# The centring of tokens in tiles 2 and 3 moved one batch of scores later, and the GpSimd chain before it recorded with priority

## The chip, the cores and the metric

The kernel runs on one core of a Trainium2 chip. Its engines are TensorE (PE in the profile; PEld is its loading of weights), VectorE (DVE), ScalarE (ACT), GpSimd (POOL) and SyncE (SP), which issues nearly all DMAs. Each engine works through its own instructions in order, and semaphores tie the engines together. The metric is the device time of one execution in microseconds, the median over several runs.

## The reference

The input is 2048 tokens of width 512 in float32. Each token is normalised, and two branches read the result: attention with 32 heads of 16 over a sliding window of 256 tokens, and a gated feed-forward net of width 1792. They meet in a product, and the input is added.

```
x = A_x
xn = _layernorm(x, axis=-1)               # (x - mean) / sqrt(var + 1e-5)
s = _A_ref(xn, A_wqkv, A_wo)              # q, k, v; windowed softmax; @ wo
g = _silu(_B_ref(xn, B_w1, B_w3, B_w2))   # (silu(xn @ w1) * (xn @ w3)) @ w2
return x + s * g
```

The part that the change touches is the layer norm: mean, variance, the reciprocal root of the variance, and the subtraction and scaling (here "centring") of every token.

## The kernel before

**Tiles.** The tokens go in four tiles t = 0 to 3 of 512, each of four blocks b of 128 tokens. A large product runs as three products of f16 halves: XH and XL are the high and low part of the normalised tokens, turned so that the features lie on partitions. The work on attention is cut into 32 units (tile, group of 8 heads, half of the group). While unit n has its softmax and its values, unit n+2 has its row maxima; beside both, a list of pieces of the other products (projections of q and k, values, feed-forward, output) is spread between them.

**Batches.** `batches` makes five or four batches of scores for a unit. A batch records some score products with their maxima (`pass1`, L661 and L675: DVE adds the mask and takes the row maximum straight from PSUM) and some of `pass2` (L742, the mask added at L749 by DVE, the exponential at L752 by ACT, the values at L770). After each batch `spread` lets pieces of the other products follow, and `step` releases work that was put off by a count of steps (`later`).

**The layer norm of tiles 1 to 3** is made beside this, by `prepare(t)` and `prepare_beside`:

- `load(b)`: four DMAs of raw tokens (L433).
- `stats(b)`: DVE, mean and variance of a block (L437, L438) into `mv`.
- `rstd(0, 4)`: three small DVE instructions make a first guess `r0` (L442 to L447), and ten GpSimd instructions on 128x4 numbers refine it (L463 to L472). The last, L472, writes `rs`.
- `centre(b)`: DVE, one instruction of 128x512 for each block (L475), which reads `mv` and `rs`.
- `turn_beside(b, n, s)`: PE turns two quarters of a block into free columns of a score bank (L513), DVE makes XH and XL from it (L522, L523).

`prepare_beside` puts stats, rstd and centre into the list `behind`. Every batch with scores ahead takes one entry from it:

```
if behind and ahead:
    with tc.issue_after(lasts["maximum"].ins):
        behind.pop(0)()
```

So an entry stands behind the last row maximum of its batch. For tile 1 the entries are pairs of blocks; for tiles 2 and 3 they are four of stats, one of rstd, four of centre and one (`turns`) that lets the turning begin; that begins when a second call, from the list of pieces, has come as well.

**What sets the order.** PE's instructions stand as written. On the other engines the order follows the place where an instruction was recorded, unless it was recorded in `urgent()`, which is `tc.high_priority(offset=200)`: such an instruction stands as if it had been recorded earlier. What empties PSUM on DVE and ACT is recorded so: L614 (the low half of a projection, `rest` in `project`; ACT makes the high half at L610), L1281 (a sum of the down product into `ACC`), L1051 and L1056 (the two gates), L749, L675, L785. PSUM has two banks, called m, for all the large products; they take turns (`bank`), so the piece after next waits until DVE or ACT has emptied its bank.

**Other lines named later.** L1257 is PE's down product, L593 the projections of q and k, L563 values, L1032 gate and up. L339 and L841 on GpSimd are its larger instructions of 128x256: the product and the casts of the normalised attention output `on`, and halves of weights. L620 and L637 are DMAs of projections to and from DRAM, L705 DMAs of row maxima into `qa`, L358 the loading of wo.

## Time and profile before

| what | us |
|---|---|
| median of 3 runs | 818.14 (816.59 to 819.52) |
| the profiled execution, its own time | 817.82 |
| its span, first to last instruction | 816.0 |
| PE busy in the span | 795.2 (97%) |
| DVE busy | 633.9 (78%) |
| ACT busy | 392.4 (48%) |
| POOL busy | 364.0 (45%) |
| mean granted PE clock | 0.998 of full speed |

The profile is of one execution. Its page gives busy times and the chain of work that ended last; the view of waits gives for each line who ended its idle time; the timeline lists instructions in order of time, with the idle time before them in brackets; the view by windows gives for stretches of time the busy time of each engine, the granted clock and the share of the DMA engines in use. All times are counted from the start of the span. Line numbers are those of the kernel before; in the changed kernel the chain and the centring stand one line further down, and everything behind `prepare_beside` three.

### The profile page before, as it was taken

How to read it: one execution, taken by the hardware profiler on the slowest of the kernel's cores; microseconds unless marked ns; L12 is line 12 of the kernel's file. 1: busy time of each engine (PE TensorE's matmuls, PEld its weight loads, DVE VectorE, ACT ScalarE, POOL GpSimd, SP SyncE). 2: the span in 40 equal slices, each digit the busy share in tenths (PEclk: the TensorE clock that was granted, in tenths of full speed). 3: DMA queues.
4: the chain of work that ended last, by engine and by line, in shares of the span. 5: the costliest groups of instructions: out<-in, count | busy, mean ns of one | idle time of the engine just before them, and what ended most of it. 6: DMA issues, size and time to landing. Idle time of an engine off the chain costs nothing.

```text
span 816.0 us, 23868 instructions
## 1 busy us (share of the span) xinstructions
PE 795.2 (97%) x9176; PEld 404.2 (50%) x9176; DVE 633.9 (78%) x2037; ACT 392.4 (48%) x591; POOL 364.0 (45%) x648
## 2 busy tenths in 40 slices
PE   8999989998999999999999999999999999999998
PEld 4434444443444444444444544456544654466465
DVE  8788788885898777787988888786777887775437
ACT  6879586563527444444444344434444334344421
POOL 2234266232328636434445264630246377560670
PEclk9999999999999999999999999999999999999999
DMA  9967554735457384666755544646362545325321
GB/s 284 258 218 254 165 179 130 276 115 188 136 141 255 105 267 120 215 180 208 204 169 171 172 100 144 168 128 189 122 197 74 161 127 149 111 77 181 111 56 70
DMA packets 109794, 134.18 MB, mean 164 GB/s; under 512 B 18864, under 2 KB 64880, under 8 KB 109680
## 3 DMA queue, kind: packets, MB, share of 16 engines
q1 hardware_dynamic: 109392, 132.13, 53.9%
q8 instruction: 72, 1.18, 0.6%
q10 hardware_dynamic: 288, 0.52, 0.2%
q14 instruction: 42, 0.34, 0.1%
HBM read 91.23 MB, written 36.57 MB: 157 GB/s over the span
## 4 chain that ended last, share of the span: by engine, by line
PE 78%; DVE 10%; ACT 5%; DMA 3%; issue 3%; SPq 1%; POOL 1%; DVEq 0%; POOLq 0%; ACTq 0%
PE m L1032 29%; PE po L770 8%; PE m L1257 8%; PE m L1175 8%; PE m L593 7%; PE s L742 5%; PE m L1309 4%; PE m L563 4%; PE s L661 3%; DVE junk L675 2%; PE po L661 2%; DMA slot<-in_A_x_dram 1%; DMA dW<-slot 1%; DVE s L749 1%; ACT slot L342 1%
## 5 line engine op out<-in xcount | busy, mean ns | idle before, releaser
L1032 PE MATMUL m<-XH,slot 128*128 128x512 f16 x896 | 267.5, 380 | 1.8 <-DVE slot L614 1.2
L752 ACT ACTIVATE pt<-s,es 128x1024 f32<-128x1024 f32 x152 | 167.6, 1112 | 198.6 <-DVE s L749 183.1
L339 POOL TENSOR_TENSOR slot<-slot,slot 128x256 f16<-128x256 f32 (+1 forms) x170 | 112.9, 691 | 218.2 <-ACT slot L1065 79.2
L1032 PEld LDWEIGHTS <-slot 128*128 128x128 f16 x1344 | 124.8, 98 | 156.2 <-issue 12.7
L1032 PE MATMUL m<-XL,slot 128*128 128x512 f16 x448 | 169.9, 379 | 0.0
L749 DVE TENSOR_TENSOR s<-s,MK 128x256 f32<-128x256 f32 (+2 forms) x280 | 118.7, 434 | 52.7 <-PE s L742 48.5
L675 DVE CUSTOM_DVE_ANT_0 junk<-s,MW 128x320 bf16<-128x320 f32 x276 | 133.9, 485 | 18.0 <-PE s L661 10.3
L675 DVE CUSTOM_DVE_ANT_0 junk<-po,MW 128x320 bf16<-128x320 f32 x172 | 83.4, 485 | 4.3
L1257 PE MATMUL m<-slot,slot 128*128 128x512 f16 x336 | 80.0, 385 | 3.6 <-DVE slot L614 3.2
L770 PE MATMUL po<-pt,V 64*32 64x320 f32 (+4 forms) x2880 | 77.2, 342 | 0.8 <-DVE pp L304 0.8
L593 PE MATMUL m<-XH,slot 128*128 128x512 f16 x240 | 71.0, 380 | 1.5 <-DVE slot L1051 0.8
L1175 PE MATMUL m<-slot,slot 128*128 128x256 f16 x588 | 68.4, 273 | 0.0
L1090 POOL TENSOR_TENSOR slot<-slot,slot 128x256 f16<-128x256 f32 x98 | 64.6, 671 | 1.1
L1047 ACT ACTIVATE slot<-m,sgs 128x512 f32<-128x512 f32 x56 | 38.3, 683 | 54.4 <-PE m L1032 53.1
L770 PEld LDWEIGHTS po<-pt,V 64*32 64x32 f32 x2880 | 50.5, 106 | 22.9 <-PE s L513 0.9
L1175 PEld LDWEIGHTS <-slot 128*128 128x128 f16 x588 | 56.1, 98 | 11.5 <-issue 2.8
L1051 DVE SCALAR_TENSOR_TENSOR slot<-slot,m 128x512 f32<-128x512 f32 x56 | 38.4, 685 | 27.9 <-ACT slot L1047 27.8
L742 PE MATMUL s<-qa,KA 50*64 50x320 f16 (+3 forms) x1472 | 58.6, 260 | 0.3 <-DVE M L675 0.2
L593 PEld LDWEIGHTS <-slot 128*128 128x128 f16 x384 | 35.6, 98 | 44.7 <-issue 3.3
L742 PEld LDWEIGHTS <-KA 50*64 50x64 f16 x1472 | 30.3, 106 | 52.5 <-issue 31.1
L1257 PEld LDWEIGHTS <-slot 128*128 128x128 f16 x336 | 30.9, 98 | 42.7 <-issue 8.9
L661 PE MATMUL s<-KA,qa 48*64 48x320 f16 (+3 forms) x824 | 45.1, 295 | 3.7 <-ACT pt L752 2.9
(188 smaller groups left out, 1095.3 us busy)
## 6 DMA issues: line engine op xcount, KB each, us to landing
slot<-dW SPq DMA_DIRECT2D x98, 256.0 KB
slot<-in_B_w_dram SPq DMA_DIRECT2D x56, 256.0 KB
slot<-dFold SPq DMA_DIRECT2D x48, 256.0 KB
dW<-slot SPq DMA_DIRECT2D x42, 256.0 KB
slot<-in_A_x_dram SPq DMA_DIRECT2D x30, 256.0 KB
KA<-dK SPq DMA_DIRECT2D x24, 288.0 KB
qa<-dQ SPq DMA_DIRECT2D x32, 192.0 KB
slot<-dWQ SPq DMA_DIRECT2D x24, 256.0 KB
```

The lines of the kernel that those rows point to most:

```text
L339: op(out[:, c], a[:, c], b[:, c])
L593: nc.tensor.matmul(cell["pp"], w[:, (a * NC + c) * P:(a * NC + c + 1) * P], b[:, c, :], start=(c, i) == parts[0][0], stop=(c, i) == parts[ ...
L661: nc.tensor.matmul(s[c:c + w, r, :n], qa[rows, 2 * p + a, ii * P + c:ii * P + c + w], ka[rows, 2 * p + a, e - n:e], start=True, stop=True)
L675: lasts["maximum"] = nc.vector.tensor_tensor_reduce(out=junk[:, :n], in0=s[:, r, :n], in1=mask, scale=1.0, scalar=NEG, op0=ALU.add, op1=AL ...
L742: nc.tensor.matmul(s[64 * h:64 * h + 64, r, o:o + 64 * n], ka[rows, 2 * p + a, 64 * (m + 4):64 * (m + 5)], qa[rows, 2 * p + a, 64 * (m + k ...
L749: nc.vector.tensor_add(v, v, MK[:, kind, of:of + n, :].unsqueeze(1).to_broadcast([P, 2 * len(which), n, 64]))
L752: lasts["exp"] = nc.scalar.activation(pt, s, AF.Exp, scale=es)
L770: nc.tensor.matmul(cell["po"][32 * i:32 * i + 32, h, 64 * (m + k):64 * (m + k + n)], V[64 * h:64 * h + 64, (4 * t + m // 2) % VB, hd * VW: ...
L1032: nc.tensor.matmul(cell[k], w[:, (a * NC + c) * P:(a * NC + c + 1) * P], b[:, c, :], start=c == 0 and i == 0, stop=c == NC - 1 and i == 2)
L1090: nc.gpsimd.tensor_sub(lo, view, hi)
L1175: nc.tensor.matmul(cell["ps"][:, c], made[:, f:f + P], wj[:, g:g + 256], start=j == j0 and c == 0 and n == 0, stop=j == j1 - 1 and n == 2, ...
L1257: nc.tensor.matmul(ps, hh[:, a * TW + b * P:a * TW + (b + 1) * P], w[:, c * D:(c + 1) * D], start=f == f0 and i == 0, stop=f == f1 - 1 and ...
```

## The change

Two edits in the layer norm of tiles 1 to 3. The ten GpSimd instructions of `rstd` are recorded in `urgent()`. And for tiles 2 and 3 an empty entry stands in `behind` after rstd, so that each of the four centrings and `turns` are taken one batch later. No instruction is added, removed or resized.

```diff
             u = lnpool.tile([P, b1 - b0], F32, name="u")
-            pool.tensor_mul(sq, r0, r0)
-            pool.tensor_mul(sq, sq, ve)
...
-            pool.tensor_mul(rs[:, b0:b1], sq, r0)
+            with urgent():
+                pool.tensor_mul(sq, r0, r0)
+                pool.tensor_mul(sq, sq, ve)
...
+                pool.tensor_mul(rs[:, b0:b1], sq, r0)
...
         work.append(lambda: rstd(0, 4))
+        if t > 1:
+            work.append(lambda: None)
         work += [lambda bs=bs: [centre(b) for b in bs] for bs in pairs]
```

The order of the instructions of PE, ACT and SP is the same in both kernels. On DVE the four centrings of tile 2 and the four of tile 3 stand later, and everything they pass moves up by one; nothing else moves. On GpSimd only the chain of tile 2 changes its place among its neighbours.

The first centring of tile 2 on DVE, before; slot_2653 is block 0 of the tokens, m_3188 the bank of a projection, m_3248 one of the down product:

```order
L675 ISA junk,M<-po,M_106 128x256
L675 ISA M 128x1
L475 TENSOR_SCALAR slot_2653<-slot_2653,mv,rs 128x512
L614 SCALAR_TENSOR_TENSOR slot_3243<-m_3188,slot_3243 128x512
L1281 SCALAR_TENSOR_TENSOR slot_1458<-m_3248,dsc,slot_1458 128x512
L749 TENSOR_TENSOR s<-s,MK 128x4x64
```

The centring stands between a row maximum and two instructions that empty the banks m. At the same place on DVE in the changed kernel (L617 is L614 of before, L1284 is L1281, L752 is L749, L678 is L675):

```order
L678 ISA junk,M<-po,M_106 128x256
L678 ISA M 128x1
L617 SCALAR_TENSOR_TENSOR slot_3242<-m_3188,slot_3242 128x512
L1284 SCALAR_TENSOR_TENSOR slot_1458<-m_3247,dsc,slot_1458 128x512
L752 TENSOR_TENSOR s<-s,MK 128x4x64
```

The two follow the maximum directly. The centring stands one batch later, where that of block 1 stood before:

```order
L678 ISA junk,M<-po,MW 128x320
L678 ISA M 128x1
L476 TENSOR_SCALAR slot_2653<-slot_2653,mv,rs 128x512
L752 TENSOR_TENSOR s<-s,MK 128x4x64
L678 ISA junk,M<-s,MW 128x320
```

Blocks 1 and 2 likewise take the places of blocks 2 and 3. The last one, block 3 (slot_2659), stood here on DVE before, inside a few small instructions on a scale `al`:

```order
L675 ISA junk,M<-s,MW 128x320
L675 ISA M 128x1
L294 TENSOR_SCALAR al<-s 128x3
L475 TENSOR_SCALAR slot_2659<-slot_2659,mv,rs 128x512
L295 SCALAR_TENSOR_TENSOR al<-s,al 128x3
L785 COPY os<-po 128x512
```

and stands now thirteen rows further on, the one place that had no centring before:

```order
L752 TENSOR_TENSOR s<-s,MK 128x2x64
L678 ISA junk,M<-s,MW 128x320
L678 ISA M 128x1
L298 TENSOR_SCALAR al<-al 128x3
L476 TENSOR_SCALAR slot_2659<-slot_2659,mv,rs 128x512
L304 TENSOR_SCALAR pp_3394<-al 128x3
```

In tile 3 the four move in the same way: the first leaves its place, three take the place of the next, and the fourth comes to stand ahead of L687.

The chain of tile 2 on GpSimd before, from its fourth instruction on; `on` is a normalised attention output:

```order
L466 TENSOR_TENSOR sq<-sq,u 128x4
L339 TENSOR_TENSOR on<-on,rb 128x256 x2
L467 TENSOR_SCALAR sq<-sq 128x4
L841 CAST slot_3259<-on 128x256
L468 TENSOR_TENSOR r_3152<-r_3152,sq 128x4
L841 CAST slot_3259<-on 128x256
L469 TENSOR_TENSOR sq<-r_3152 128x4
L339 TENSOR_TENSOR slot_3259<-on,slot_3259 128x256
L470 TENSOR_TENSOR sq<-sq,ve 128x4
L339 TENSOR_TENSOR slot_3259<-on,slot_3259 128x256
L471 TENSOR_SCALAR sq<-sq 128x4
L472 TENSOR_TENSOR rs<-sq,r_3152 128x4
```

and in the changed kernel (the chain is L464 to L473, L844 is L841 of before):

```order
L339 TENSOR_TENSOR on<-on,rb 128x256
L468 TENSOR_SCALAR sq<-sq 128x4
L339 TENSOR_TENSOR on<-on,rb 128x256
L469 TENSOR_TENSOR r_3152<-r_3152,sq 128x4
L844 CAST slot_3258<-on 128x256
L470 TENSOR_TENSOR sq<-r_3152 128x4
L844 CAST slot_3258<-on 128x256
L471 TENSOR_TENSOR sq<-sq,ve 128x4
L339 TENSOR_TENSOR slot_3258<-on,slot_3258 128x256
L472 TENSOR_SCALAR sq<-sq 128x4
L339 TENSOR_TENSOR slot_3258<-on,slot_3258 128x256
L473 TENSOR_TENSOR rs<-sq,r_3152 128x4
```

Each large instruction has gone behind one instruction of the chain more, but all six still stand between the fourth instruction of the chain and its last, in both kernels. The chains of tiles 1 and 3 have kept their places.

More of the change, by code (lines that the diff above doesn't have):

```diff
@@ L462, in rstd @@
             u = lnpool.tile([P, b1 - b0], F32, name="u")
-            pool.tensor_mul(sq, r0, r0)
-            pool.tensor_mul(sq, sq, ve)
-            pool.tensor_scalar(u, sq, -10 / 3, None, op0=ALU.add)
-            pool.tensor_mul(sq, sq, u)
-            pool.tensor_scalar(sq, sq, 5.0, None, op0=ALU.add)
-            pool.tensor_mul(r0, r0, sq)
-            pool.tensor_mul(sq, r0, r0)
-            pool.tensor_mul(sq, sq, ve)
-            pool.tensor_scalar(sq, sq, -0.5 * (3 / 8)**3 * XS, 1.5 * (3 / 8) * XS, op0=ALU.mult, op1=ALU.add)
-            pool.tensor_mul(rs[:, b0:b1], sq, r0)
+            with urgent():
+                pool.tensor_mul(sq, r0, r0)
+                pool.tensor_mul(sq, sq, ve)
+                pool.tensor_scalar(u, sq, -10 / 3, None, op0=ALU.add)
+                pool.tensor_mul(sq, sq, u)
+                pool.tensor_scalar(sq, sq, 5.0, None, op0=ALU.add)
+                pool.tensor_mul(r0, r0, sq)
+                pool.tensor_mul(sq, r0, r0)
+                pool.tensor_mul(sq, sq, ve)
+                pool.tensor_scalar(sq, sq, -0.5 * (3 / 8)**3 * XS, 1.5 * (3 / 8) * XS, op0=ALU.mult, op1=ALU.add)
+                pool.tensor_mul(rs[:, b0:b1], sq, r0)
         def centre(b):
```

## The prediction

> **What bounds the kernel now.** The page first: TensorE (PE) is busy for nearly the whole span and fills most of the chain that ended last, so only what makes PE wait, or slows its clock, is worth anything.

> ```profile
> PE 795.2 (97%) x9176; PEld 404.2 (50%) x9176; DVE 633.9 (78%) x2037; ACT 392.4 (48%) x591; POOL 364.0 (45%) x648
> PE 78%; DVE 10%; ACT 5%; DMA 3%; issue 3%; SPq 1%; POOL 1%; DVEq 0%; POOLq 0%; ACTq 0%
> ```

> The view of waits says whom PE waits for (total, times, longest). I quote PE's two longest rows and the centring's own:

> ```profile
> PE m L1257 <- DVE slot L614: 3.2, 1, 3.2
> PE s L661 <- ACT pt L752: 2.9, 3, 1.6
> DVE slot L475 <- POOL rs L472: 3.8, 2, 3.4
> ```

> PE's longest single wait, 3.2 us, is for a projection's bank to be emptied by L614. And DVE has one wait of 3.4 us ahead of a centring. The timeline shows that the two are one event, in tile 2 (start, length, instruction, idle before):

> ```profile
> 184.60 0.20 POOL L463 TENSOR_TENSOR sq<-r 128x4 f32<-128x4 f32 x1 [8.11 <-DVE r L447]
> 185.80 1.42 POOL L339 TENSOR_TENSOR on<-on,rb 128x256 f32<-128x256 f32 x2
> 190.40 0.20 POOL L472 TENSOR_TENSOR rs<-sq,r 128x4 f32<-128x4 f32 x1
> 187.14 0.08 DVE L675 DVE_READ_ACCUMULATOR2_ANT M<- 128x1 f32 x1
> 190.63 0.55 DVE L475 TENSOR_SCALAR slot<-slot,mv,rs 128x512 f32<-128x512 f32 x1 [3.40 <-POOL rs L472]
> 191.09 0.68 DVE L614 SCALAR_TENSOR_TENSOR slot<-m,slot 128x512 f16<-128x512 f32 x1
> 187.09 0.59 ACT L610 ACTIVATE slot<-m 128x512 f16<-128x512 f32 x1
> 186.52 2.10 PE L1257 MATMUL m<-slot,slot 128*128 128x512 f16 x9
> 191.83 2.72 PE L1257 MATMUL m<-slot,slot 128*128 128x512 f16 x6 [3.20 <-DVE slot L614]
> ```

> GpSimd's chain ends at 190.60. DVE is free at 187.2 but has the centring next, waits for `rs`, and only then reaches L614, whose input from ACT was there at 187.68. PE has used up its other bank at 188.62 and stands until 191.83, when L614 has ended.

> The stall has a second price. Six of these products normally take 1.40 us, here 2.72; the rows below are from the chain of waits, the windows give busy times by engine, PE's granted clock and the DMA share:

> ```profile
> 85.48 1.40 PE m L1257 x6
> 191.83 2.72 PE m L1257 x6
> 194.55 0.57 PE s L742 x7
> 198.70 0.35 PE s L742 x8
> ```

> ```profile
> 191.20:191.80 0.60, 0.00 (x0) 0.00 (x0) 0.60 (x2) 0.00 (x0) 0.00 (x0) 0.80 0.04 10
> 191.80:194.50 2.70, 2.67 (x10) 0.74 (x9) 0.63 (x1) 0.00 (x0) 0.00 (x0) 0.50 0.67 232
> 195.20:196.00 0.80, 0.80 (x12) 0.36 (x5) 0.80 (x4) 0.00 (x0) 0.00 (x0) 1.00 0.95 351
> 54.00:57.00 3.00, 1.97 (x9) 0.68 (x7) 2.89 (x9) 2.90 (x7) 2.10 (x4) 1.00 0.73 249
> 55.64 0.59 PE L1032 MATMUL m<-XH,slot 128*128 128x512 f16 x2 [1.03 <-DVE slot L614]
> ```

> The granted clock falls to half only in the last part of the idle time (0.80 as a mean from 191.20 to 191.80) and is whole again from 195.20. A wait of 1.03 us at 55.64 left it at 1.00. [...]

> **The change part by part.**

> *Priority of the chain: nothing.* The ten small instructions keep all six large ones (on L339 and L841) ahead of the last, L472. I take `rs` to end at 190.60 as before; that GpSimd runs the six in a slightly other order moves the output of `on` by one small instruction, 0.2 us, and it is read only by the output product, units later. In tiles 1 and 3 the chain hasn't moved. So the first edit is worth 0.

> *First centring of tile 2, one batch later: the gain.* L614 no longer stands behind `rs`. It starts when ACT's half is there, 187.09 + 0.59 = 187.68. From the start of L614 to PE's start took 191.83 - 191.09 = 0.74, so the bank is free at 188.42. PE ends its nine products at 188.62 by the model. The wait of 3.20 is gone whole, with 0.2 us to spare; if the handover is worse than that by another 0.3, so much of the gain is lost. What then comes next on DVE, L1281, needs those nine products and stands at 188.6, as PE goes on.

> *The clock.* Without the idle time there is no half clock: 2.72 - 1.40 = 1.32 on the six products and 0.57 - 0.35 = 0.22 on L742 behind them, 1.54 together.

> *Where the centrings go.* The first now stands at the second one's old place, at 198.01:

> ```profile
> 198.01 0.54 DVE L475 TENSOR_SCALAR slot<-slot,mv,rs 128x512 f32<-128x512 f32 x1
> 201.67 0.54 DVE L475 TENSOR_SCALAR slot<-slot,mv,rs 128x512 f32<-128x512 f32 x1
> 209.12 0.63 DVE L298 TENSOR_SCALAR al<-al 128x3 int32<-128x3 int32 x1
> 216.80 0.69 DVE L614 SCALAR_TENSOR_TENSOR slot<-m,slot 128x512 f16<-128x512 f32 x1 [1.63 <-ACT slot L610]
> 203.50:215.00 11.50, 11.50 (x152) 5.73 (x145) 10.63 (x41) 6.33 (x10) 3.29 (x6) 1.00 0.32 86
> ```

> Shifted by the gain (3.20 + 1.54 = 4.74) that place is at 193.3, and `rs` was ready at 190.6: no wait, with 2.7 us to spare. Three of the four fill places that had a centring. The net addition is one centring behind L298, at 209.1 before the shift. It holds DVE 191.09 - 190.63 = 0.46 us, in a stretch where DVE is busy 10.63 of 11.50. Behind it are L1051 and L1056, which empty banks for PE; PE is busy 11.50 of 11.50 there, so it doesn't wait for either now, and at 216.80 DVE idles 1.63. Cost between 0 and 0.46; I take 0, since that idle time swallows it.

> *Tile 3.* Its chain isn't disturbed, and the centring doesn't wait:

> ```profile
> 409.09 0.20 POOL L472 TENSOR_TENSOR rs<-sq,r 128x4 f32<-128x4 f32 x1
> 410.69 0.54 DVE L475 TENSOR_SCALAR slot<-slot,mv,rs 128x512 f32<-128x512 f32 x1
> 428.03 0.30 DVE L687 TENSOR_SCALAR NM<-M 128x16 f16<-128x16 f32 x1
> 434.53 0.43 DVE L749 TENSOR_TENSOR s<-s,MK 128x256 f32<-128x256 f32 x1 [1.03 <-PE s L742]
> ```

> `rs` is there 1.4 us before the centring, so nothing is gained. The last centring now stands ahead of L687 and delays what follows by 0.46, until DVE's idle 1.03 at 434.5. Again 0 to 0.46, and I take 0.

> *The sum.* 817.82 (the profiled execution: span 816.0 and 1.82 around it) - 3.20 - 1.54 = 813.08. The median of the runs shown is 818.14, 0.32 above; with it **813.4**. From the bounds (0.3 of handover, twice 0.46) at worst 814.6 (813.4 + 0.3 + 0.92).

> **The rivals.**

> *A. Only the idle time is saved, about 814.9.* The half clock is seen in one execution, and there it set in just before the idle time was over; in other executions of before the same stall may have ended with the clock whole. The 1.54 was then not in the median, and what goes is 818.14 - 3.20 = 814.94. For: the three runs spread from 816.59 to 819.52, wider than 1.54. Against: the median is above the profiled execution, not 1.54 below. [...]

> *B. The wait moves to a transfer, about 817.8.* PE comes 4.7 us sooner to data that arrive at a fixed time. The issues just before the stall, and the share of the DMA engines after it:

> ```profile
> 186.41 2.77 SPq L705 DMA_DIRECT2D qa<-mt  x4
> 189.22 0.44 SPq L637 DMA_DIRECT2D qa<-dQ  x1
> 191.80 0.39 SPq L620 DMA_DIRECT2D dK<-slot  x1
> 194.24 1.99 SPq L358 DMA_DIRECT2D slot<-in_A_wo_dram  x4
> 198.60:203.50 4.90, 4.90 (x45) 2.18 (x44) 3.66 (x13) 3.10 (x5) 0.00 (x0) 1.00 0.83 297
> 206.97 0.34 PE s L742 x8
> ```

> The maxima and q for the next unit go out by 189.7, and PE reads them at 206.97, then at 202.2. If they came only at 207, nothing would be won. Against: they are ahead of the large block of transfers (L358 and what follows), with 12 us to go. That block itself is held up by L614 through L620 and moves ahead with PE. The same time would come out if the change didn't do what it says, that is if something else held L614 to 191.

> *C. Slower, about 824: the turning overtakes the centring.* PE's order hasn't moved, so each L513 (turning a block) stands where it stood, while the centrings come a batch later: from 198.01 to 201.67, 3.7 us. If the distance from a block's last instruction on DVE to its L513 were smaller than that, PE would stand about 3.7 us with the half clock's 1.54 behind it, 5.2 in each of two tiles: 818.14 - 4.74 + 10.4 = 823.8. It decides from the point where the distance is under one batch:

> ```profile
> 216.56 0.23 PE s L513 x16
> 441.39 0.42 DVE L522 CAST XH<-s 128x256 f16<-128x256 f32 x1
> ```

> Against it: the first L513 of tile 2 is at 216.56 and even the last centring stands at about 209.8 on the same scale; in tile 3 the first turned quarter is read at 441.39, the last centring stands at 428.

> **How the numbers follow.** Forecast 0.65, A 0.14, B 0.13, C 0.08 (with any other loss of more than the gain). A measurement of this kernel tells 0.3% from no change, about 2.5 us: faster is below 815.7. The forecast and most of A lie below: 0.76 faster. B and a badly measured rest of A give 0.16 for the same, C 0.08 for slower. The forecast's own range is 812.3 to 814.9. The range from 812.2 (the whole gain, and medians of three runs that spread by 2.9 us) to 816.4 takes in A and the upper ends of all costs, and leaves out C and most of B.

> **What would show it.** In the new profile: no wait of PE for the projection's L614 near 188, and no row of a centring's wait for `rs` over 1 us; granted clock 1.00 through 188 to 196, and a mean of 1.000 rather than 0.998; six products of L1257 in 1.40 there; the first centring near 193 without idle time ahead of it; L472 (then L473) still near 190.6; all later stages about 4.7 us sooner. I am wrong if PE stands elsewhere for over 1 us between 188 and 216, if it waits at an L513, or if the clock halves at another place.

## The result, and the profile after

| | us |
|---|---|
| before, median of 6 runs | 818.08 (816.59 to 819.52) |
| changed kernel, median of 6 runs | 813.25 (813.02 to 813.40) |
| ratio, with its 95% interval | 0.9938 (0.9928 to 0.9947) |
| the changed kernel's profiled execution, and its span | 813.03, 811.2 |

The change gained 4.83 us, and the runs agree far better than before. At the place of the old stall the timeline of the changed kernel reads as follows (start, length, instruction, idle before):

```profile
187.10 0.59 ACT L613 ACTIVATE slot<-m 128x512 f16<-128x512 f32 x1
187.73 0.69 DVE L617 SCALAR_TENSOR_TENSOR slot<-m,slot 128x512 f16<-128x512 f32 x1 [0.49 <-ACT slot L613]
188.68 0.75 DVE L1284 SCALAR_TENSOR_TENSOR slot<-m,dsc,slot 128x512 f32<-128x512 f32 x1 [0.26 <-PE m L1260]
186.53 3.40 PE L1260 MATMUL m<-slot,slot 128*128 128x512 f16 x15
190.40 0.20 POOL L473 TENSOR_TENSOR rs<-sq,r 128x4 f32<-128x4 f32 x1
193.17 0.54 DVE L476 TENSOR_SCALAR slot<-slot,mv,rs 128x512 f32<-128x512 f32 x1
204.83 0.53 DVE L476 TENSOR_SCALAR slot<-slot,mv,rs 128x512 f32<-128x512 f32 x1
```

L617, which empties the projection's bank, waits for ACT alone and starts at 187.73 instead of 191.09. PE runs its nine and the next six down products as one group of fifteen. GpSimd's chain ends as late as before, but the first centring comes only at 193.17 and doesn't wait. The granted clock (the number three from the right in the view by windows) stays whole:

```profile
189.00:190.00 1.00, 1.00 (x9) 0.34 (x11) 0.43 (x1) 0.00 (x0) 0.84 (x3) 1.00 0.02 4
191.00:192.00 1.00, 1.00 (x7) 0.41 (x6) 1.00 (x6) 0.59 (x1) 0.00 (x0) 1.00 1.02 336
193.00:194.00 1.00, 1.00 (x14) 0.38 (x15) 0.71 (x3) 0.09 (x1) 0.00 (x0) 1.00 0.98 219
```

In the view of waits the old first row of PE is gone, the second is now the first, and the longest wait of a centring is one of 0.4 us, in tile 1:

```profile
PE s L664 <- ACT pt L755: 2.9, 3, 1.6
DVE slot L476 <- POOL rs L473: 0.4, 1, 0.4
```

All of the gain is made at this one place: the nine products ahead of the stall start at 186.52 before and, in the group of fifteen, at 186.53 after. Near the end of the program, 24 products of the output projection, before and then after:

```profile
801.52 5.34 PE L1309 MATMUL m<-slot,slot 128*128 128x512 f16 x24
```

```profile
796.68 5.34 PE L1312 MATMUL m<-slot,slot 128*128 128x512 f16 x24
```

That is 4.84 us earlier; at the three products that follow the stall (195.29 before, 190.46 after) it was 4.83. Nothing was given back in the 600 us between.

### The profile page after: what moved, and what is told of

The parts are those of the page before. It is cut to its first block, busy times and chain, and to the rows that moved or that the text cites. A ratio compares the mean times of both kernels' runs of the same rounds, so it can differ in the third digit from the quotient of the medians.

```text
span 811.2 us, 23867 instructions
## 1 busy us (share of the span) xinstructions
PE 794.5 (98%) x9176; PEld 404.2 (50%) x9176; DVE 634.2 (78%) x2037; ACT 392.5 (48%) x591; POOL 364.0 (45%) x648
## 4 chain that ended last, share of the span: by engine, by line
PE 80%; DVE 9%; ACT 5%; issue 3%; DMA 2%; SPq 0%; DVEq 0%; POOL 0%; ACTq 0%
PE m L1035 30%; PE po L773 8%; PE m L1260 8%; PE m L1178 8%; PE m L596 7%; PE s L745 5%; PE m L1312 4%; PE m L566 4%; PE s L664 3%; DVE junk L678 2%; PE po L664 2%; ACT sqa L249 1%; ACT slot L342 1%; ACT pt L755 1%; DMA dW<-slot 1%
## 5 line engine op out<-in xcount | busy, mean ns | idle before, releaser
L755 ACT ACTIVATE pt<-s,es 128x1024 f32<-128x1024 f32 x152 | 167.7, 1113 | 192.8 <-DVE s L752 174.6
L339 POOL TENSOR_TENSOR slot<-slot,slot 128x256 f16<-128x256 f32 (+1 forms) x170 | 113.2, 694 | 212.2 <-ACT slot L1068 85.0
L752 DVE TENSOR_TENSOR s<-s,MK 128x256 f32<-128x256 f32 (+2 forms) x280 | 118.8, 435 | 50.7 <-PE s L745 46.4
L678 DVE CUSTOM_DVE_ANT_0 junk<-s,MW 128x320 bf16<-128x320 f32 x276 | 133.9, 485 | 18.0 <-PE s L664 10.3
L678 DVE CUSTOM_DVE_ANT_0 junk<-po,MW 128x320 bf16<-128x320 f32 x172 | 83.5, 485 | 4.3
```

Of the source, the lines that this page charges most:

```text
L339: op(out[:, c], a[:, c], b[:, c])
L678: lasts["maximum"] = nc.vector.tensor_tensor_reduce(out=junk[:, :n], in0=s[:, r, :n], in1=mask, scale=1.0, scalar=NEG, op0=ALU.add, op1=AL ...
L752: nc.vector.tensor_add(v, v, MK[:, kind, of:of + n, :].unsqueeze(1).to_broadcast([P, 2 * len(which), n, 64]))
L755: lasts["exp"] = nc.scalar.activation(pt, s, AF.Exp, scale=es)
```

## The experiments

The theories: (1) the wait of the first centring of tile 2, ahead of a bank's emptying in DVE's order, is the whole loss; (2) the priority brings part of the gain; (3) tile 3 brings part; and on the price of the stall, (1a) idle time costs itself and a half clock comes only behind a long one, against (1b) any such wait halves the clock.

**Each part of the change by itself.** The priority alone:

```diff
-            pool.tensor_mul(sq, r0, r0)
...
+            with urgent():
+                pool.tensor_mul(sq, r0, r0)
...
```

> The priority of the chain alone, centrings as before. Theory 1 (the first centring of tile 2 holds the bank's emptying back until rs is there): rs still ends near 190.4 us, PE waits about 3.2 us near 188 and the clock halves behind it; 818.1 us. Theory 2 (the priority brings part of the gain): between 813.3 and 817, with a shorter wait.

Measured: 818.05 us, ratio 1.0001 (0.9987 to 1.0015). `rs` ended at 190.72 and the stall was there:

```profile
190.52 0.20 POOL L473 TENSOR_TENSOR rs<-sq,r 128x4 f32<-128x4 f32 x1
191.96 1.94 PE L1258 MATMUL m<-slot,slot 128*128 128x512 f16 x6 [3.21 <-DVE slot L615]
```

The later centring alone:

```diff
         work.append(lambda: rstd(0, 4))
+        if t > 1:
+            work.append(lambda: None)
```

> The later centring alone, the chain without priority. Theory 1: all of the gain, 813.25 us, clock 1.000, no wait of PE near 188. Theory 2: some of the gain is missing, above 814 us.

Measured: 813.18 us, ratio 0.9941 (0.9922 to 0.9959). And in one tile each, `t == 2` and `t == 3` in place of `t > 1`:

> Later centring in tile 2 alone, no priority. Theory 1: 813.25 us. Theory 3 (tile 3's centrings bring a part as well): about 815 to 816 us. If tile 3's late centrings cost their 0.46 us, this is up to 0.46 faster than the change, 812.8.

> Later centring in tile 3 alone, no priority. Theory 1: as before, 818.1 us, with the same wait and half clock in tile 2. Theory 3: below 817 us.

Measured: tile 2 alone 813.15 us (0.9940, 0.9921 to 0.9959), tile 3 alone 818.29 us (1.0000, 0.9985 to 1.0015). Theories 2 and 3 fall: the priority alone leaves the wait and the time as they were, tile 3 brings nothing that these runs can tell, and the late centrings of tile 3 cost nothing that can be seen (813.18 with them, 813.15 without).

**Is it the lateness of rs, and not the centring's place?** Here the centring stays in front of the bank's emptying, and GpSimd's large instructions are moved from between the chain's steps to behind it:

```diff
-                later(3, multiply)
+                later(8 if (t, g) == (0, 1) else 3, multiply)
```

> Centrings where they were before, the chain without priority; instead the product of one attention output (its DMAs, the two large products, and so the casts and differences behind them) is put off by five steps, so that GpSimd has the chain of tile 2 without a large instruction in it. Theory 1 (the lateness of rs is the six large instructions): rs near 187.4 us instead of 190.6, PE waits 0.2 us or less, clock 1.000, 813.2 to 813.6 us, as fast as the change without moving a centring. Theory 4 (the position of the centring itself, its 0.46 us ahead of the bank's emptying, costs): about 813.7 us.

Measured: 813.30 us, ratio 0.9935 (0.9920 to 0.9949). The timeline of this kernel:

```profile
187.22 0.20 POOL L472 TENSOR_TENSOR rs<-sq,r 128x4 f32<-128x4 f32 x1
187.99 1.41 POOL L339 TENSOR_TENSOR on<-on,rb 128x256 f32<-128x256 f32 x2 [0.56 <-DMA qa<-mt]
187.46 0.55 DVE L475 TENSOR_SCALAR slot<-slot,mv,rs 128x512 f32<-128x512 f32 x1 [0.18 <-POOL rs L472]
186.57 3.54 PE L1257 MATMUL m<-slot,slot 128*128 128x512 f16 x15
```

The ten steps end 3.2 us sooner, and with them the stall ends, though no centring has moved. So the six large instructions inside the chain are what made `rs` late. This is the other cure, as fast as the change (their ranges, 813.09 to 813.49 and 813.02 to 813.40, overlap), and it is what the priority might be thought to do. Theory 4's 813.7 was missed: a centring in front of the bank's emptying costs nothing that can be told when it waits as little as here (0.18 us).

**The price of the stall.** Three kernels with the centrings as before and another length of chain. In the first, tile 2's second refinement is left out; the second adds one multiplication by 1 to that (its edit isn't shown); the third keeps the whole chain and adds six. The added lines of the first and the third:

```diff
+            if t == 2:
+                pool.tensor_scalar(rs[:, b0:b1], r0, (3 / 8) * XS, None, op0=ALU.mult)
+            else:
...
```

```diff
+            for _ in range(6 if t == 2 else 0):
+                pool.tensor_scalar(sq, sq, 1.0, None, op0=ALU.mult)
             pool.tensor_mul(rs[:, b0:b1], sq, r0)
```

> Centrings where they were before; in tile 2 the chain's second refinement is left out (four instructions become one scaling), so tile 2's normalisation is that of one step less. By the old rows rs ends near 188.64 instead of 190.60, PE's wait is about 1.3 us instead of 3.2. Theory 1a (idle time costs itself, a half clock comes only behind a long one): 813.25 + 1.3 = 814.5 us, clock 1.000, and runs that agree within 0.5 us. Theory 1b (any such wait brings the half clock, 1.5 us): 816.0 us.

> As the short chain, with one extra multiplication by 1 in it, which stands behind one more large instruction of GpSimd: rs near 189.4, PE's wait about 2.1 us. Theory 1a with a limit above 2.1: 815.3 us, clock 1.000, narrow spread. If the limit lies below 2.1: 816 to 818 us, with a spread of some us between runs, since the length of the half clock would depend on the moment.

> Centrings and chain as before, with six extra multiplications by 1 ahead of the chain's last instruction in tile 2: rs some 1.75 us later, PE's wait about 5.0 us. Idle time alone: 818.1 + 1.75 = 819.8 us if the clock's price stays what it was on average (1.6 us). If a longer wait makes the half clock surer or longer: up to 821.5 us. If the length of the half clock is a matter of the moment, the runs spread by 1 us or more, as before's do (816.59 to 819.52).

Their profiles give PE's wait, in this order:

```profile
190.73 1.46 PE L1260 MATMUL m<-slot,slot 128*128 128x512 f16 x6 [1.63 <-DVE slot L617]
```

```profile
191.25 2.28 PE L1262 MATMUL m<-slot,slot 128*128 128x512 f16 x6 [2.45 <-DVE slot L619]
```

```profile
193.45 2.72 PE L1259 MATMUL m<-slot,slot 128*128 128x512 f16 x6 [5.04 <-DVE slot L616]
```

The waits came out longer than I had worked out (1.63 for 1.3, 2.45 for 2.1). With the wait of 1.63 us the clock stayed whole at the stall and behind it:

```profile
188.00:192.00 4.00, 2.37 (x12) 0.87 (x9) 2.14 (x3) 0.16 (x1) 2.55 (x6) 1.00 0.25 83
192.00:196.00 4.00, 4.00 (x34) 1.73 (x33) 3.33 (x12) 1.12 (x1) 0.00 (x0) 1.00 0.95 309
```

Each execution also has its mean granted clock. A mean below 1.000 says that the clock was lower somewhere, not that it was at the stall: in this profiled execution (mean 0.999) the clock is 1.00 in every window of 20 us up to 800 us, and 0.92 only from 800 to 820, some 600 us behind the stall, and with tile 2 alone an execution of 813.06 us had a mean of 0.997. So the table gives the times beside the means; the row on before takes the 44 executions that ran beside the experiments:

| PE's wait in the profile | executions | times at a mean clock of 1.000 | times below that |
|---|---|---|---|
| none (the change, 6) | 6 | 813.03 to 813.30 | 813.02, 813.40 (0.999) |
| 1.63 | 6 | 814.99 | 815.07 to 815.50 (0.998, 0.999) |
| 2.45 | 12 | 7: 815.82 to 816.00 | 5: 816.13 to 819.40 |
| 3.20 (before) | 44 | 10: 816.34 to 817.21 | 34: 817.76 to 820.82 |
| 5.04 | 6 | none | 820.06 to 821.49 |

At 1.63 us the median is 815.12, 1.87 above the change: the idle time and little else, and theory 1b's 816.0 is missed by all six. At 2.45 the median is 815.94; seven executions kept the full clock, and four (817.36 to 819.40) stand at least 1.36 above them. The fifth, 816.13, lies so close to the seven that its half clock probably stood elsewhere; no profile shows it. At 3.20 time and mean go together: ten of 44 kept the full clock, and the 34 others begin 0.55 above the last of them. The median of the ten, 816.65, is 3.40 above the change, and that of the 34, 818.22, is 1.57 higher still. At 5.04 none kept it; the median, 820.58, is 0.8 above the 819.8 expected from the longer idle time alone. So 1a holds, but with no sharp limit: in these four kernels, the longer the wait, the surer the half clock (by the times, none of 6 executions, 4 or 5 of 12, 34 of 44, 6 of 6). Its middle price here, 1.57, is what the profile of before had shown (1.54).

**More lateness, and tile 1.** Two empty entries for one; then one entry in tile 1 too (`t > 0`):

> Two empty entries in tiles 2 and 3 instead of one, no priority; the turning begins one place later as well. Theory 1 (only the wait mattered, further lateness is free): 813.2 us. If late centrings cost (the slower rival of the prediction): 813.5 us and more, with a wait of PE at the turning or at the emptying of a bank.

> The empty entry in tile 1 as well, no priority. In the profile of the change a centring of tile 1 waits 0.4 us for rs. Theory 1: PE didn't wait behind it, so 813.2 us. If that wait reached PE: 812.8 us. Tile 1's turning moves one place later too, and PE waits for DVE several times there: a loss of up to 1 us is possible.

Measured: two batches 813.40 us (0.9938, 0.9921 to 0.9954), tile 1 too 813.66 us (0.9939, 0.9925 to 0.9954). Two batches are still free to within what can be told here; its profile shows PE's waits as they were, and none at a turning. With tile 1 the wait of 0.4 us went, but PE got a longer one, from tile 1's turned blocks, a place later too:

```profile
PE m L595 <- DVE XH L522: 2.4, 1, 2.4
```

In this execution the wait cost nothing: it took 813.00 us, PE had run 0.8 us ahead of the change's own profile before the wait (the first of these products at 158.91 and 159.74) and was level with it soon behind (169.31 and 169.34). The kernel's four runs spread from 813.00 to 814.42; what the two slower ones (814.25, 814.42) lost stays open, as neither has a profile. No version tried is clearly faster than the change.

## Why the prediction was right, point by point

- *Priority of the chain, 0:* right. The first experiment shows it alone at 1.0001, and in the changed kernel `rs` still ends at 190.60. The chain doesn't get past the six large instructions by it, and they are the cause of the lateness, as moving them shows.
- *The idle time, 3.20:* right, and 0.2 short. The bank's emptying started at 187.73, worked out as 187.68, with PE never standing. In executions of before that kept the full clock the stall cost 3.40.
- *The clock, 1.54:* right for the middle, and mis-stated as a fixed price. It is 0 in 10 of 44 executions and about 1.6 in most; the eight from 819.02 up lie over 2.3 above the median of the ten, and no profile shows why. Rival A thus did occur, with too small a share to move the median: the stall left the clock whole in about a quarter of the executions, and the argument against it, that the median lies above the profiled execution, was the one that counted. The spread of 2.9 us in the runs of before went with the stall: without it the six runs lie within 0.38.
- *The centrings' new places, 0:* right. The first came at 193.17 (predicted 193.3) without waiting, the last at 204.83, and PE's waits from there to the end are those of before, none over 0.4 us. Tile 3 with and without the late centrings differs by 0.03 us.
- *Rival B, a transfer at a fixed time:* ruled out; a DMA ends no wait of PE over 0.6 us, and the shift stays 4.83 to the end.
- *Rival C, the turning overtaken by the centring:* didn't occur even at two batches. With one empty entry the turning is set by the other call and keeps its place (PE's order is unchanged), the centrings still well ahead of it; with two entries `turns` becomes the later call and the turning moves along with the centrings (its first products in tile 2 start at 216.43 instead of 211.55). Tile 1 shows the kind of wait that C had in mind, 2.4 us of PE waiting for a turned block, though there by moving the turning itself, and at no cost in the execution that was profiled.
- *The sum, 4.74:* 4.83 was measured. So close a hit is partly luck: a median of six executions of before depends on how many of them kept the full clock, and the time of one ran from 816.34 to 820.82.

## What to carry to other kernels

On an engine that works in order, as DVE did here (a bank's emptying whose input was there at 187.68 started at 191.09, behind the centring), look at what stands behind a waiting instruction: the wait of a small side job (here 3.4 us of DVE for 128x4 numbers from GpSimd) cost 0.6% because a PSUM bank was to be emptied behind it. Either cure was enough: placing the consumer later, behind what others wait for, or clearing the producer's queue of large instructions. The raised priority did neither here, and the order showed that before any run. Where PE idled 3.20 us here, 34 of 44 executions had the half clock as well, about 1.6 us more: count it as a chance, and take a wide spread of run times (2.9 us here, 0.38 without the stall) as a hint of such a place.

## What the runs showed of the hardware

```profile
190.00:192.00 2.00, 0.04 (x1) 0.04 (x1) 1.24 (x3) 0.00 (x0) 0.72 (x2) 1.00 0.33 98
192.00:193.00 1.00, 1.00 (x5) 0.49 (x5) 0.56 (x1) 0.00 (x0) 0.00 (x0) 0.90 0.13 48
193.00:196.00 3.00, 3.00 (x24) 0.97 (x22) 1.31 (x6) 0.40 (x1) 0.00 (x0) 0.50 0.96 288
196.00:197.00 1.00, 1.00 (x5) 0.43 (x4) 0.62 (x1) 0.72 (x1) 0.00 (x0) 0.90 1.05 406
```

All four are 3.4 us. In the last the clock fell only at 192.8, 0.8 us after PE was back at work at 191.96; in before it fell 0.27 us ahead of PE's return at 191.83. With the wait of 5.04 us it was low from 191.9 to 198.7, 6.8 us, twice as long:

```profile
191.40:191.90 0.50, 0.00 (x0) 0.00 (x0) 0.00 (x0) 0.00 (x0) 0.41 (x2) 1.00 0.00 0
191.90:192.40 0.50, 0.00 (x0) 0.00 (x0) 0.14 (x1) 0.00 (x0) 0.24 (x2) 0.50 0.00 0
198.50:199.00 0.50, 0.50 (x3) 0.16 (x2) 0.34 (x1) 0.50 (x1) 0.00 (x0) 0.77 1.10 377
```

The start doesn't follow the idle time's own: counted from the end of the nine products ahead of the stall, the clock fell after 2.9 us in before and with the wait of 2.45 us, after 3.5 with the wait of 5.04, and after 4.1 with the priority alone. What sets the moment no run shows. A second dip was seen as well: in the kernel with the priority alone the clock was at half from about 121.1 to 124.5, 3.4 us again, behind a wait of PE of 1.63 us in a sparse stretch (PE busy 0.49 us in the microsecond ahead of 119, 0 in the next). In the profile of before the same wait (1.62) left the clock at 1.00. The dip cost next to nothing, as the nine products ahead of the stall start at 186.64 with it and at 186.52 in before.

```profile
119.00:120.00 1.00, 0.00 (x0) 0.00 (x0) 0.11 (x2) 1.00 (x3) 1.00 (x3) 1.00 0.29 105
121.00:122.00 1.00, 1.00 (x6) 0.37 (x4) 0.93 (x5) 1.00 (x3) 0.12 (x1) 0.55 0.01 2
124.00:125.00 1.00, 1.00 (x5) 0.35 (x3) 0.17 (x1) 1.00 (x4) 0.43 (x1) 0.74 0.03 8
```

What stays open is why some executions of before took 819 to 820.8 us: no profile caught one.
